# Changing when PV is held back beside full-array matmuls, the order of FFN blocks and two scheduler constants, in an attention + FFN kernel

## The chip, the cores and the metric

One core of a Trainium2 chip runs the whole program in one launch. The metric is device time in microseconds (us). Engines are named as in the profile: PE is TensorE's matmuls, PEld its weight loads, ACT is ScalarE, DVE is VectorE. "Before" and "after" are the two kernels. A ratio is the mean time of one kernel's fast runs over that of the other's fast runs of the same rounds, so it is not quite the ratio of the medians quoted.

## The reference, cut to what matters

```python
def reference(A_x, A_wqkv, A_wo, B_x, B_w1, B_b1, B_w2, B_b2):   # S=2048, D=1024, F=3584, 32 heads of 32
    q, k, v = split(layernorm(A_x) @ A_wqkv)
    p = softmax(q @ k.T * 32 ** -0.5)          # 32 heads x 2048 x 2048
    h = A_x + (p @ v) @ A_wo
    return h + gelu(layernorm(h) @ B_w1 + B_b1) @ B_w2 + B_b2
```

## The kernel before

The kernel isn't written in instruction order. It builds a graph of tasks, and a list scheduler with a cost table puts each engine's tasks in order at build time; that order is then fixed. Attention runs in eight chunks of 256 query rows. A chunk has eight *jobs* (one for each group of four heads), a job eight *rounds*. In a round PE makes eight score matmuls (QK, row-tiled, kind `qk`), ACT two exponentials, and PE eight PV matmuls and four of the softmax denominator (both column-tiled, kind `pv`). All other matmuls are *background*, in groups that need a PSUM bank each: first the K, Q and V projections, then per chunk the output projection (`wo`), `ffn1` of chunk c-1 and `ffn2` of chunk c-2. `ffn1` and the V projection run on the full array, most of the rest column-tiled.

```python
def round(self):                                   # one round of a job
    pe(fns, 0.217, ..., kind="qk", mode="row")     # scores of 8 matmuls
    act(... ACT.Exp ...)                           # twice; occ = EXP[q]
    pe(fns, 0.217, ..., kind="pv", mode="col")     # PV
    ...                                            # denominator, one round later
...
PLAN = [F2[0], 3, F2[1], 4, F2[2], 5, F2[3], 2]    # order of ffn2 groups and ffn1 blocks
...
pool_of = {7: [], 4: [], 6: B_ps[6].w + B_ps[6].r} # banks of jobs and background; 4 only in the lead-in
PV_START = 6
HOLD = 3

def full_array(t):                                 # ffn1 and V projections
    return t.alt is not None and t.grp.name[:2] in ("f1", "pv")

def pick_pe(rd, now, state, up):                   # what PE does next
    ...                                            # waiting: rounds whose P is ready and whose PV isn't done
    if qk is not None:
        return qk
    if pv is not None and not (state["mode"] == "full" and bg is not None and full_array(bg[1]) and waiting < HOLD):
        job = job_of.get(pv)
        if job is None or job.bank is not None:
            return pv
        if free and pv is pvs[n] and (waiting >= PV_START or last or bg is None):
            job.bank = free[0]                     # the job takes its PSUM bank here
            ...
            return pv
    if bg is not None:
        ...
        return t
```

The last-but-one group, ffn2 of chunk 6, can start only when all of chunk 6's ffn1 and its tanh have been placed.

The softmax here doesn't subtract the row's maximum and nothing guards it: scores larger than these inputs give would overflow.

## Time and profile before

| | before |
|---|---|
| time, median of three runs | 1099.68 us (1098.5 to 1100.67) |
| profiled span, mean granted clock | 1096.5 us, 0.997 |
| busy: PE, PEld, DVE, ACT | 1062.1, 589.0, 822.9, 1021.6 us |
| last QK starts, chunk 7's ffn1 starts | 1019.87, 1044.95 us |
| last matmul of chunk 6's ffn1 | 998.7 us |

The page has busy time per engine, the chain of work that ended last, and groups of instructions; the timeline lists an engine's instructions in order, with the idle time before each in brackets and what ended it. The lines themselves stand in the prediction.

### The profile page before, as it was taken

Reading aid. Unit: us, or ns where it says so; the run is one execution under the profiler, and the core shown is the slowest. Engines: PE = TensorE matmul, PEld = TensorE weight load, DVE = VectorE, ACT = ScalarE, POOL = GpSimd, SP = SyncE. Lnnn points to the kernel's source line nnn. Section 1 sums busy time; section 2 is a strip of 40 time slices with the busy share of each in tenths; the row PEclk is TensorE's granted clock in tenths of the full one; section 3 lists DMA queues with packets and bytes.
Section 4 is the critical chain, followed back from the end, with each engine's and each line's share of the span. In section 5 each row is a group of like instructions: output and inputs, shape, how many; then the busy total and the mean of one; then the engine's idle time right before and its main releaser. Section 6 shows DMA issues by size and latency. Waiting matters only on the chain.

```text
span 1096.5 us, 41949 instructions
## 1 busy us (share of the span) xinstructions
PE 1062.1 (97%) x19130; PEld 589.0 (54%) x19135; DVE 822.9 (75%) x1449; ACT 1021.6 (93%) x1135; POOL 17.8 (2%) x33
## 2 busy tenths in 40 slices
PE   7999999999999989999999999999999999999999
PEld 6545555554444655554555455455545544554485
DVE  7456666767767998788788788877887888887562
ACT  5889999999999999999999999999999999999351
POOL 1000000000000000000000000000000000000000
PEclk9999999999999999999999999999999999999999
DMA  7960100013444755577838856765778477968860
GB/s 197 195 159 3 51 3 3 3 41 92 120 122 127 210 133 162 183 242 150 271 113 254 218 169 185 210 208 153 234 162 255 136 224 205 311 186 261 248 224 20
DMA packets 269211, 176.52 MB, mean 161 GB/s; under 512 B 51434, under 2 KB 265066, under 8 KB 269034
## 3 DMA queue, kind: packets, MB, share of 16 engines
q1 hardware_dynamic: 269034, 173.84, 55.4%
q8 instruction: 150, 2.46, 0.9%
q14 instruction: 27, 0.22, 0.1%
HBM read 155.98 MB, written 11.01 MB: 152 GB/s over the span
## 4 chain that ended last, share of the span: by engine, by line
ACT 83%; PE 15%; DMA 1%; DVE 1%; issue 0%; POOL 0%; POOLq 0%; DVEq 0%
ACT PT L709 79%; PE ps L505 8%; ACT a_sq L850 4%; PE ps L502 3%; PE ps L701 1%; PE ps L721 1%; DMA hnT<-xb 1%; PE ps L907 1%; PE ps L740 1%; DVE PS L716 0%; ACT xnT L584 0%; PE ps L581 0%; DVE gT L851 0%; ACT V L592 0%; DVE a_os L878 0%
## 5 line engine op out<-in xcount | busy, mean ns | idle before, releaser
L709 ACT ACTIVATE PT<-ps 128x1024 bf16<-128x1024 f32 x1024 | 953.8, 1164 | 12.7 <-PE ps L701 12.4
L716 DVE TENSOR_TENSOR PS<-PT 128x1024 bf16<-128x1024 bf16 x495 | 327.6, 686 | 83.1 <-ACT PT L709 49.5
L701 PE MATMUL ps<-QT,KT 32*128 32x256 bf16 x4096 | 203.9, 273 | 13.5 <-ACT PT L709 11.5
L505 PE MATMUL ps<-hnT,w1r 128*128 128x256 bf16 x1632 | 209.5, 274 | 2.1 <-DVE gT L832 0.6
L502 PE MATMUL ps<-w2r,gT 128*32 128x512 bf16 x2880 | 192.8, 383 | 1.9 <-issue 0.8
L721 PE MATMUL ps<-PT,V 128*32 128x256 bf16 x4096 | 180.9, 275 | 5.9 <-ACT PT L709 5.0
L505 PEld LDWEIGHTS ps<-hnT,w1r 128*128 128x128 bf16 x1632 | 146.2, 98 | 57.0 <-issue 36.2
L701 PEld LDWEIGHTS ps<-QT,KT 32*128 32x128 bf16 x4096 | 61.3, 92 | 163.5 <-ACT PT L709 141.7
L740 PE MATMUL ps<-PS,ones 128*32 128x256 bf16 x1980 | 139.4, 276 | 2.3 <-DVE PS L716 1.5
L502 PE MATMUL ps<-xnT,Wall 128*32 128x512 bf16 x1888 | 126.0, 381 | 1.3 <-DVE stg L594 1.2
L721 PEld LDWEIGHTS ps<-PT,V 128*32 128x32 bf16 x4096 | 94.4, 96 | 54.5 <-ACT PT L709 24.0
L502 PEld LDWEIGHTS ps<-w2r,gT 128*32 128x32 bf16 x2880 | 67.4, 96 | 71.2 <-issue 26.7
L832 DVE TENSOR_TENSOR gT<-ps,b1f 128x512 bf16<-128x512 f32 x98 | 67.4, 687 | 25.7 <-PE ps L505 24.5
L740 PEld LDWEIGHTS ps<-PS,ones 128*32 128x32 bf16 x1980 | 51.7, 96 | 40.6 <-DVE PS L716 23.4
L505 PE MATMUL ps<-Wall,xnT 128*128 128x128 bf16 (+1 forms) x896 | 69.3, 227 | 0.7 <-ACT xnT L584 0.7
L851 DVE SCALAR_TENSOR_TENSOR gT<-a_sq,gT 128x1024 bf16<-128x1024 bf16 x49 | 59.9, 1222 | 12.3 <-ACT a_sq L850 11.8
L502 PEld LDWEIGHTS ps<-xnT,Wall 128*32 128x32 bf16 x1888 | 43.5, 96 | 46.5 <-issue 15.0
L505 PEld LDWEIGHTS ps<-Wall,xnT 128*128 128x128 bf16 x896 | 55.2, 98 | 16.3 <-issue 10.7
L502 PE MATMUL ps<-w1r,OT 128*32 128x512 bf16 x896 | 62.2, 381 | 0.5 <-DVE OS L752 0.2
L848 DVE SCALAR_TENSOR_TENSOR a_sq<-a_sq,gT 128x1024 bf16<-128x1024 bf16 x49 | 59.8, 1221 | 0.7
L850 ACT ACTIVATE a_sq<-a_sq 128x1024 bf16<-128x1024 bf16 x49 | 58.9, 1203 | 0.0
L749 DVE STREAM_TRANSPOSE DT<-ps 128x256 f32<-128x256 f32 x64 | 28.5, 445 | 20.1 <-PE ps L740 20.1
(76 smaller groups left out, 570.7 us busy)
## 6 DMA issues: line engine op xcount, KB each, us to landing
w2r<-in_B_w_dram SPq DMA_DIRECT2D x105, 512.0 KB, 6.0
w1r<-in_B_w_dram SPq DMA_DIRECT2D x102, 512.0 KB, 4.6
w1r<-in_A_wo_dram SPq DMA_DIRECT2D x28, 512.0 KB, 4.4
wk<-in_B_w_dram SPq DMA_DIRECT2D x9, 512.0 KB, 5.9
xrb<-in_A_x_dram SPq DMA_DIRECT2D x16, 256.0 KB, 4.9
Wall<-in_A_wqkv_dram SPq DMA_DIRECT2D x16, 256.0 KB, 5.1
wv<-in_B_w_dram SPq DMA_DIRECT2D x8, 512.0 KB, 6.9
a_x<-in_A_x_dram SPq DMA_DIRECT2D x28, 128.0 KB, 3.4
```

Source lines behind the costliest of these rows:

```text
L502: fns.append(lambda p, j=j: p.matmul(dst(32 * j, 32 * j + 32), lhsT[:, 32 * j:32 * j + 32], rhs, start=start, stop=stop, tile_position=(0, ...
L505: t.alt = [lambda p: p.matmul(dst(0, P), lhsT, rhs, start=start, stop=stop, skip_group_check=True)]
L701: fns.append(lambda p, i=i, hh=hh, r0=r0: p.matmul(psum[:, 2 * us[hh // 2] + hh % 2, 256 * i:256 * i + 256], KT[r0:r0 + 32, g, 256 * r + P ...
L709: t = act(lambda a, u=u, q=q: a.activation(PT[:, s, 2 * q:2 * q + 2, :], psum[:, 2 * u:2 * u + 2, :], ACT.Exp, bias=0.0, scale=SCALE), 102 ...
L716: dve(lambda v: v.tensor_tensor(PS[:, z, :, :], PT[:, s, :, 0:256], PT[:, s, :, 256:512], ALU.add), c_dve(1024, 2), reads=B_PT[s], writes= ...
L721: fns.append(lambda p, i=i, hh=hh: p.matmul(psum[32 * hh:32 * hh + 32, self.bank, 0:256], V[:, g, 2 * r + i, 32 * hh:32 * hh + 32], PT[:, ...
L740: fns.append(lambda p, i=i, hh=hh, src=src: p.matmul(psum[32 * hh:32 * hh + 32, self.bank, 256:512], ones32[:, :], src[:, hh, :], start=False,
L749: dve(lambda v: v.transpose(DT[f][:], psum[:, self.bank, 256:512]), c_dve_ps(256), reads=[self.buf], writes=[B_DT[f]], prio=-1)
L832: gate[c] = dve(lambda v, xh=xh, fc=fc, grp=grp: v.tensor_tensor(xh, psum[:, grp.bank, :].rearrange("p (f n) -> p f n", f=2), b1f[:, fc:fc ...
L848: dve(lambda v: v.scalar_tensor_tensor(v4(sq), v4(sq), C2, xh, ALU.add, ALU.mult), c_dve(n), reads=[b_sq] + b_xh, writes=[b_sq], prio=GP)
L850: gate[c] = act(lambda a: a.activation(sq, sq, ACT.Tanh, bias=0.0, scale=K2 / 2), n, writes=[b_sq], prio=-1, kind="tanh")
L851: t = dve(lambda v: v.scalar_tensor_tensor(xh, v4(sq), 1.0, xh, ALU.add, ALU.mult), c_dve(n), reads=[b_sq] + b_xh, writes=b_xh, prio=GP)
```

## The change

Its intent, in its author's words: PV is held back while a full-array ffn1 group has work, until three rounds of P wait, so that PV runs in longer column-tiled stretches. Four lines differ (three edits: the *rule*, the *plan*, and the *constants* of the cost table).

```diff
-    EXP = (0.9163, 0.9013)
+    EXP = (0.9161, 0.9011)
...
-    PLAN = [F2[0], 3, F2[1], 4, F2[2], 5, F2[3], 2]
+    PLAN = [F2[0], 2, F2[1], 6, F2[2], 5, F2[3], 1]
...
-        if pv is not None and not (state["mode"] == "full" and bg is not None and full_array(bg[1]) and waiting < HOLD):
+        if pv is not None and not (bg is not None and not last and full_array(bg[1]) and waiting < HOLD):
...
-    gr.schedule(pick_pe, switch=0.11382196630878494)
+    gr.schedule(pick_pe, switch=0.10231147062341138)
```

## The prediction

> **What bounds the kernel now.** I read four views: the busy table and clock, the chain of waits, every ACT idle gap, and the PE timeline where chunks change.
>
> ```profile
> PE 1062.1 (97%) x19130; PEld 589.0 (54%) x19135; DVE 822.9 (75%) x1449; ACT 1021.6 (93%) x1135; POOL 17.8 (2%) x33
> ...
> ACT 83%; PE 15%; DMA 1%; DVE 1%; issue 0%; POOL 0%; POOLq 0%; DVEq 0%
> ...
> L709 ACT ACTIVATE PT<-ps 128x1024 bf16<-128x1024 f32 x1024 | 953.8, 1164 | 12.7 <-PE ps L701 12.4
> ```
>
> PE and ACT both look full, but 83% of the chain that ended last is ACT, nearly all of it the softmax exponentials. They waited only 12.7 us in total. The ACT timeline says where these gaps lie: after the exponential that starts at 63.26 us only four gaps over 0.05 us remain before the exponentials end: 0.28, 0.39, 0.88 and 1.40 us, 2.95 us together. (The others lie in the first 63 us, in the lead-in, which the changed rule doesn't touch: its matmul groups are named neither ffn1 nor V projection.) Two of these gaps and the end of attention:
>
> ```profile
> 818.93 21.20 ACT L709 ACTIVATE PT<-ps 128x1024 bf16<-128x1024 f32 x23 [0.88 <-PE ps L701]
> 1009.56 11.11 ACT L709 ACTIVATE PT<-ps 128x1024 bf16<-128x1024 f32 x12 [1.40 <-PE ps L701]
> ```
>
> So from 63 to about 1022 us ACT sets the pace: 330 exponentials took 302.67 us in the chain (63.26 to 366), 0.917 us each. The change removes no exponential. After 1022.5 us the bound is PE. The tail, by the PE timeline:
>
> ```profile
> 1023.48 0.81 PE L505 MATMUL ps<-wk,OT 128*128 128x512 bf16 x3 [0.16 <-issue]
> ...
> 1030.25 1.89 PE L505 MATMUL ps<-w2r,gT 128*128 128x512 bf16 x8
> 1031.97 0.61 PE L581 MATMUL ps<-ident,xbl 128*128 128x128 bf16 x8
> 1032.42 2.97 PE L505 MATMUL ps<-w2r,gT 128*128 128x512 bf16 x12
> 1035.22 0.61 PE L581 MATMUL ps<-ident,xbl 128*128 128x128 bf16 x8
> 1035.67 9.44 PE L505 MATMUL ps<-w2r,gT 128*128 128x512 bf16 x42
> 1044.95 1.91 PE L505 MATMUL ps<-hnT,wk 128*128 128x256 bf16 x16
> ```
>
> The reader sees the last output projection (1023.48 to 1030.25), then 62 matmuls of the second FFN product (ffn2) of chunk 6, left over from attention, then ffn1 of chunk 7 from 1044.95. The ACT timeline has the last hnT copy at 1035.87, 1.02 us long, so ffn1 could start at 1036.89. The leftover is useful filler up to there; behind it, 1044.95 - 1036.89 = 8.06 us are pure backlog on the path. **This 8 us and the 2.95 us of ACT gaps are all that PE scheduling can give back.** The rest of the tail, ffn1 and ffn2 of chunk 7, is back-to-back full-array work.
>
> [...]
>
> ```profile
> 1014.50 0.33 PE ps L701 x8
> 1014.83 1.41 PE ps L502 x24
> 1016.24 0.33 PE ps L701 x8
> 1016.57 1.62 PE ps L502 x28
> 1018.19 0.33 PE ps L701 x8
> 1018.52 0.55 PE ps L502 x8
> 1019.07 0.44 PE ps L721 x16
> ```
>
> Eight PV matmuls (L721, column-tiled, behind column-tiled ffn2) take 0.44/2 = 0.22 us; eight QK matmuls (L701, row-tiled, 256 columns too) between column-tiled ones take 0.33, so one change costs 0.11 us. The ffn2 pieces confirm it: 28 less 24 is 0.21 for four, so eight should take 0.42 and take 0.55 after QK. [...] The trace has 917, and I use 917: ACT has no slack hidden between its instructions. [...] PE's 97% is not proof that PE is the bound; the chain decides, and it says ACT until 1022.
>
> **The change, part by part.** No instruction is added or removed; the order on PE changes, and with it DMA and DVE order. The diff has four edits.
>
> (1) The rule. Before, a ready PV was held back only when PE stood in full-array mode. QK comes once a round, every two exponentials (1.83 us), puts PE in row mode, and so lets PV through right behind it. Once in column mode, PV drained until none was left. After, PV is held in any mode while a full-array ffn1 or V-projection group is next and fewer than three rounds of P wait. Read literally, this removes the after-QK visits with one or two rounds waiting, but also removes the hysteresis: after one PV the count falls from 3 to 2 and the hold is on again. A job (8 rounds) still starts only at six waiting. Before, it drains six and then takes one or two more visits. After, it drains four, and then gets one round at a time. The PE records of the last chunk (905 to 1023 us) hold 134 mode changes and 13 column stretches of PV or its denominator alone beside ffn1: 5 between row and full (10.5 rounds of PV), 4 between full and row, 4 between two QKs. After the change I count, as an estimate: 224 ffn1 matmuls of 0.1095 us (1.91 us for 16 in the tail timeline, less overlap: 1.75/16) are 24.5 us, at about 1.2 us of free PE time a round some 20 rounds, up to one visit each. A visit in the middle of ffn1 costs two changes, one behind QK only one. Worst case 40 changes against about 20 now: 20 x 0.11 = **+2.2 us** of PE time in the last chunk. If the visits merge as intended, some 6 to 10 fewer: **-0.7 to -1.1 us**.
>
> (2) The order. PV yields to ffn1, so ffn1 of chunk 6 can end earlier by the PVs deferred: two to three rounds of PV and denominator at 0.33 us, 0.7 to 1.0 us. This matters, because ffn2 of chunk 6 may start only when the last tanh of ffn1 has been placed: ffn1's last matmuls start at 997.58, the tanh at 1004.21, ffn2 at 1004.86; in between PE had only attention, with waits of 0.29, 0.41, 0.52 and 0.41 us (1.63 in all). The deferred PVs fill these. Worth **-0.7 to -1.6 us** of the 8 us backlog.
>
> (3) The plan of blocks, from 3, 4, 5, 2 to 2, 6, 5, 1. Now the first three ffn1 blocks alternate with pieces of ffn2 (16 ffn1 matmuls, then 4 to 12 of ffn2, three times at 929 to 937 us). One block fewer in that place takes out one alternation, 2 to 4 changes: **-0.2 to -0.4 us**. The last ffn1 pair ends at about the same time.
>
> (4) The constants of the scheduler's cost tables (exponential 0.2 ns shorter, mode change 0.102 for 0.114) cost nothing on the chip, but can flip ties anywhere. This is luck of placement: 1 or 2 us either way.
>
> Only what falls in the last chunk moves the end by the backlog; in earlier chunks PE time hides beside ACT, as the four small gaps show. Sum with the middle of each: (1) between +2.2 and -0.9, say +0.5; (2) -1.1; (3) -0.3; ACT gaps 2.95 us, of which I let a third be recovered, -1. That is -1.9 us. From the median 1099.68 I predict **1097.8 us**.
>
> **The rivals.** *A: visits multiply.* PE needs 2 to 4 us more, the backlog of 8 us grows to 12, and QK is sometimes late: 1103 to 1105 us. For it: the missing hysteresis; against it: PE still has waits of 1.63 us in the last chunk, and attention work has first call. *B: the backlog goes.* Changes fall enough to put 4 to 8 us more of ffn2 ahead of attention's end: 1090 to 1094 us. For it: 134 changes x 0.11 = 14.7 us of the last chunk are changes, so a tenth fewer is 1.5 us; against it: two changes per QK can't go, and QK is most of them (64 rounds). *C: nothing visible.* ACT hides all of it, within 1.5 us of now. *D: ACT starves on P slots.* Eight slots of P, six of which wait when a job starts; PV held longer keeps two more filled and its PSUM bank occupied for some two rounds more, so a late bank would stop exponentials. For it: 0.88 us of gap already at 818.93 with column work before it; against: the hold ends at three waiting, well under eight. It would make 1105 to 1115 us.
>
> **Range and chances.** C and a weak B are likeliest; A next. The floor, if all backlog and all gaps went, is 1099.68 - 8.06 - 2.95 = 1088.7, which is 1.0% below: faster by over 2% (1077.7) is out of reach unless ACT itself gets quicker. Slower by over 2% (1121.7) needs 22 us, which only D could make. Range 1091.5 to 1103.5 us; faster 0.01, within 2% 0.975, slower 0.015.
>
> **What would show it right or wrong.** Exponentials still 0.917 us and their gaps after 63 us under 4 us in sum: the bound stands. Mode changes in the last chunk counted from the PE records: below 134 is the intent, above is A. The start of chunk 7's ffn1 after the end of the last hnT copy: under 8.06 us is gain, over it loss, and the total should move by that plus the shift of attention's end. ffn2 of chunk 6 should start 1 us or so earlier against the end of ffn1. The prediction is wrong if ACT gains gaps over 5 us, if the tail after the last QK shrinks by more than the backlog, or if the lead-in's 63 us move.

The price of a mode change is read from the fence of seven lines (1014.50 to 1019.07 us), and the 917 ns are the 302.67 us of 330 exponentials.

## More of the kernel before

Scores use six of the eight PSUM banks that the kernel allocates (`B_ps`), so after the lead-in two banks are left, 6 and 7. An open job holds one of them until its result is copied out, and background groups then share the other.

Time differences in the experiments are differences of the two medians, unless a profile's span is named.

## The result

After took **1103.69 us** (median of four, 1103.22 to 1104.29), before 1099.74 (1098.5 to 1100.67): ratio 1.0037, interval 1.002 to 1.0054. That is "within 2%", as forecast, but 0.2 us above the range, and slower where I had said faster.

The page of after, the three lines that answer to the first fence of the prediction:

```profile
PE 1063.7 (97%) x19126; PEld 591.2 (54%) x19126; DVE 821.8 (75%) x1449; ACT 1022.9 (93%) x1135; POOL 16.9 (2%) x33
...
ACT 66%; PE 32%; DVE 1%; issue 1%; POOL 0%; DVEq 0%; POOLq 0%
...
L709 ACT ACTIVATE PT<-ps 128x1024 bf16<-128x1024 f32 x1024 | 952.8, 1123 | 14.4 <-PE ps L701 14.0
```

Busy times are the same within 2.2 us: no work came or went. But PE's share of the chain that ended last is 32% in place of 15%: the exponentials often depend on PE now. The ACT timeline of after between 400 and 460 us, where before shows no gap of this kind:

```profile
417.69 1.02 ACT L709 ACTIVATE PT<-ps 128x1024 bf16<-128x1024 f32 x1 [0.61 <-PE ps L701]
421.64 1.06 ACT L850 ACTIVATE a_sq<-a_sq 128x1024 bf16<-128x1024 bf16 x1 [0.15 <-DVE a_sq L848]
425.76 6.65 ACT L709 ACTIVATE PT<-ps 128x1024 bf16<-128x1024 f32 x7 [0.32 <-PE ps L701]
445.88 7.50 ACT L709 ACTIVATE PT<-ps 128x1024 bf16<-128x1024 f32 x8 [0.60 <-PE ps L701]
```

Three of these wait for QK and one for DVE; more gaps before exponentials follow at 604, 647, 807 and 840 us. The end, from after's PE timeline:

```profile
1028.16 1.04 PE L505 MATMUL ps<-wk,OT 128*128 128x512 bf16 x4
...
1035.15 1.89 PE L505 MATMUL ps<-w2r,gT 128*128 128x512 bf16 x8
...
1037.33 2.54 PE L505 MATMUL ps<-w2r,gT 128*128 128x512 bf16 x11
...
1040.15 10.52 PE L505 MATMUL ps<-w2r,gT 128*128 128x512 bf16 x48
1050.51 1.91 PE L505 MATMUL ps<-hnT,wk 128*128 128x256 bf16 x16
```

The last output projection starts at 1028.16 (before 1023.48), and 67 matmuls of leftover ffn2 follow (before 62). The last hnT copy ends at 1041.37 (its ACT record: 1040.35, 1.02 us long), so the backlog on the path is 1050.51 - 1041.37 = 9.14 us (before 8.06). From the start of chunk 7's ffn1 to the end both take 51.6 us.

So the profiled span grew by 5.6 us: attention ends later (last exponential starts at 1026.18, before 1021.33: +4.85), the stretch from there to the end of the last hnT copy is 0.37 shorter, and the backlog is 1.08 larger. The 4.85 splits by the ACT records into three. The first exponential after the lead-in starts 1.47 later. The gaps after it sum to 4.96 us in place of 3.00 (+1.96). The remaining 1040 operations took 919.7 ns each in place of 918.3 (+1.4: waits too short to show as gaps). Of after's gaps, those at 418, 422, 426, 446, 604, 647, 807 and 840 us came back in its control run e1 within 0.5 us of their place (all gaps of e1 sum to 4.4 us); what e14, the control of before, shows stands below.

### The profile page after: what moved, and what is told of

Its sections match the earlier page's. It is cut to its first block, busy times and chain, and to the rows that moved or that the text cites. A ratio compares the mean times of both kernels' runs of the same rounds, so it can differ in the third digit from the quotient of the medians.

```text
span 1102.1 us, 41919 instructions
## 1 busy us (share of the span) xinstructions
PE 1063.7 (97%) x19126; PEld 591.2 (54%) x19126; DVE 821.8 (75%) x1449; ACT 1022.9 (93%) x1135; POOL 16.9 (2%) x33
## 3 DMA queue, kind: packets, MB, share of 16 engines
q8 instruction: 150, 2.46, 0.9%
## 4 chain that ended last, share of the span: by engine, by line
ACT 66%; PE 32%; DVE 1%; issue 1%; POOL 0%; DVEq 0%; POOLq 0%
ACT PT L709 62%; PE ps L502 11%; PE ps L505 11%; PE ps L701 4%; ACT a_sq L850 3%; PE ps L721 3%; PE ps L740 2%; PE ps L907 1%; DVE stg L594 0%; DVE PS L716 0%; ACT xnT L584 0%; DVE a_sq L848 0%; DVE gT L851 0%; PE ps L581 0%; DVE gT L832 0%
## 5 line engine op out<-in xcount | busy, mean ns | idle before, releaser
L709 ACT ACTIVATE PT<-ps 128x1024 bf16<-128x1024 f32 x1024 | 952.8, 1123 | 14.4 <-PE ps L701 14.0
L505 PE MATMUL ps<-hnT,w1r 128*128 128x256 bf16 x1632 | 214.3, 275 | 4.5 <-DVE gT L832 2.5
L721 PEld LDWEIGHTS ps<-PT,V 128*32 128x32 bf16 x4096 | 98.2, 96 | 49.6 <-ACT PT L709 20.4
L505 PE MATMUL ps<-Wall,xnT 128*128 128x128 bf16 (+1 forms) x896 | 72.2, 229 | 2.8 <-DVE V L594 1.9
L749 DVE STREAM_TRANSPOSE DT<-ps 128x256 f32<-128x256 f32 x64 | 28.5, 445 | 20.6 <-PE ps L740 20.5
```

The costliest lines, as they stand in the source:

```text
L505: t.alt = [lambda p: p.matmul(dst(0, P), lhsT, rhs, start=start, stop=stop, skip_group_check=True)]
L709: t = act(lambda a, u=u, q=q: a.activation(PT[:, s, 2 * q:2 * q + 2, :], psum[:, 2 * u:2 * u + 2, :], ACT.Exp, bias=0.0, scale=SCALE), 102 ...
L721: fns.append(lambda p, i=i, hh=hh: p.matmul(psum[32 * hh:32 * hh + 32, self.bank, 0:256], V[:, g, 2 * r + i, 32 * hh:32 * hh + 32], PT[:, ...
L749: dve(lambda v: v.transpose(DT[f][:], psum[:, self.bank, 256:512]), c_dve_ps(256), reads=[self.buf], writes=[B_DT[f]], prio=-1)
```

## The experiments

All kernels gave correct results. Two theories stood at the start. **Theory 1, background work left undone:** the time follows how much background matmul work is still undone when attention ends, plus ACT gaps. **Theory 2, mode changes:** each change of tiling mode costs 0.11 us (in before, the first matmul of a new mode ends 0.21 us after the last of the old one with 256 columns, and 0.32 with 512, where 0.108 and 0.2155 are usual); the program of after has 1255, that of before 1215 (the single PE records agree with the program). A third, chance in the clock, was to be told apart by controls. The background work done by a given moment is worked out from the PE records: each matmul counted at 0.2155 us per 512 columns, the usual step from end to end in the records (half for 256, a quarter for each column-tiled piece), and compared with the first profile of before at the same round of attention (round 512 is the last).

### The three edits alone, and the control

**e1_after_again** is after unaltered; **e2_rule_only**, **e3_plan_only** and **e4_constants_only** are before with one edit each, as in the diff above.

> The changed kernel unaltered, as a control: how far do its lead-in, its clock dips and its gaps repeat? Theory 1 (backlog and ACT gaps): 3.5 to 4.5 us over the kernel before, of which about 1.7 us is backlog (the program has 77 matmuls of chunk 6's ffn2 behind the last QK, 69 before; 8 x 0.2155) and 1.5 to 2 us ACT gaps that repeat at the same places (418, 426, 446, 647, 807, 840 us). Theory 2 (mode changes): its 40 more changes cost 4.4 us. Theory 3 (clock dips, chance): lead-in 1.5 us longer than before only in the first profile, not here, and 2 to 3 us over before.

> Only the hold rule, with the old plan and constants. The program has 112 matmuls of chunk 6's ffn2 behind the last QK (all four groups) in place of 69, and 1273 mode changes in place of 1215. Theory 1: +43 x 0.2155 = +9.3 us, so about 1109. Theory 2: +58 x 0.11 = +6.4 us at most, about 1106. If the rule as such is harmless and the plan or constants did the harm: 1098 to 1101.

> Only the plan 2, 6, 5, 1, with the old rule and constants. 102 matmuls behind the last QK (+33), 1196 mode changes (-19). Theory 1: +33 x 0.2155 = +7.1 us, about 1107. Theory 2: -2 us or nothing. The two differ in sign here.

> Only the two constants of the cost tables, with the old rule and plan. 75 matmuls behind the last QK (+6), 1206 mode changes (-9). Theory 1: +1.3 us, 1101, plus or minus what the ACT gaps do. Theory 2: -1 us.

| run | median us | before in the same rounds | ratio (interval) |
|---|---|---|---|
| e1 after again | 1102.29 | 1097.73 | 1.0040 (1.0022 to 1.0057) |
| e2 rule | 1116.95 | 1097.73 | 1.0176 (1.0157 to 1.0194) |
| e3 plan | 1112.09 | 1097.73 | 1.0123 (1.0104 to 1.0142) |
| e4 constants | 1106.03 | 1097.73 | 1.0070 (1.0054 to 1.0086) |

Each edit alone is *worse* than all three together. Theory 2 falls: plan and constants have 19 and 9 fewer mode changes and are 14.4 and 8.3 us slower. Theory 1 has the signs right and the sizes too small (+9.3, +7.1 and +1.3 expected from the program, +19.2, +14.4 and +8.3 measured). The traces say why. When the matmuls of each chunk's ffn1 were through, in us:

| ffn1 of chunk | 0 | 1 | 2 | 5 | 6 | last QK |
|---|---|---|---|---|---|---|
| before | 397.0 | 490.1 | 589.6 | 896.4 | 998.7 | 1019.9 |
| after | 405.1 | 504.6 | 606.2 | 906.0 | 1005.6 | 1024.7 |
| e1 after again | 405.1 | 504.7 | 606.2 | 905.6 | 1005.3 | 1024.4 |
| e2 rule only | 410.8 | 509.0 | 611.4 | 920.2 | 1025.3 | 1019.4 |
| e3 plan only | 397.3 | 491.4 | 591.4 | 891.6 | 1012.0 | 1024.0 |

With the rule, ffn1 is already 8 to 14 us late at its *first* chunk and stays late to the end. In background work: the rule alone is 3.5 us behind before at round 128, 7.6 at round 192 (the end of the projection stage, with most of chunk 0's ffn1 done too), 12.0 at round 288, and still 13.0 at the last QK. A lag made early need not be hidden beside ACT.

It isn't that PE has no time to spare. Behind chunk 0's ffn1, PE of before has no background matmul for 9.2 us:

```profile
396.65 0.61 PE L505 MATMUL ps<-hnT,w1r 128*128 128x256 bf16 x4
...
406.16 2.67 PE L505 MATMUL ps<-hnT,w1r 128*128 128x256 bf16 x17
```

In between it does attention's matmuls and waits for exponentials; the next chunk's ffn1 needs an hnT that is filled again only when this ffn1 is through. In after the same hole lies from 405.1 to 415.85. At round 202, inside it, after, e9 and e10 have made good all of their lag. When ffn1 ends late, the hole and all behind it start late, so that after is 5.4 us behind again at round 206 and 7.3 at round 256. Nor is a lag always carried to the end: after is 1.0 us behind at round 448. e5, which differs from it by the plan alone, is 7.9 behind there, so the new plan pays this back. But attention of after is then 6.0 us late itself.

In e2 ffn1 of chunk 6 then isn't through when attention ends, and ffn2 of chunk 6 can't fill the wait for the last layer norm. From its PE timeline:

```profile
1022.70 2.90 PE L505 MATMUL ps<-hnT,w1r 128*128 128x256 bf16 x25
1025.44 1.03 PE L505 MATMUL ps<-wk,OT 128*128 128x512 bf16 x4
...
1036.19 1.03 PE L581 MATMUL ps<-ident,xbl 128*128 128x128 bf16 x8 [1.82 <-DVE xbl L574]
1037.02 19.91 PE L505 MATMUL ps<-w2r,gT 128*128 128x512 bf16 x80
1056.77 0.93 PE L505 MATMUL ps<-hnT,wk 128*128 128x256 bf16 x7
```

ffn1 of chunk 6 ends behind the last QK (1019.37), PE idles, and all of ffn2 of chunk 6 lies on the path: 18.5 us from the last hnT copy to the next ffn1, before 8.06. In e3 the loss is in the last chunk. Its background was 1.6 us *ahead* of before at round 448 and is 7.1 behind at the last QK; PE's idle gaps from round 448 to the last QK sum to 13.2 us, before 5.3.

### Pairs

**e5_rule_constants** has rule and constants with the old plan, **e6_plan_constants** is after without the rule, **e13_rule_plan** has rule and plan with the old constants. With these all eight combinations are measured.

> Rule and constants, old plan. Theory 1 (the time follows how much background matmul work is still undone when the last QK is issued, plus gaps): 112 matmuls of chunk 6's ffn2 left in the program (before 69), so at least +9.3 us, 1107 to 1113. It shares its program with the changed kernel up to the middle of chunk 3's attention, so the lag of background work at round 192 should again be 3.6 us, not the 7.6 of the rule alone. Theory 2 (mode changes, 62 more x 0.11): +6.8 us. The clock dip at 20 us seen in both profiles of the changed kernel should be here too if the program makes it; it is chance if it isn't here.

> The changed kernel without the rule. If the rule is what makes the changed kernel slow, this one is at 1097 to 1099. Theory 1: 84 left in the program (+15 x 0.2155 = +3.2 us), and the last chunk idles on PE as in the plan-only and constants-only runs (rest of 15 to 20 us after round 448 in place of 10), so 1104 to 1109, slower than the changed kernel: the rule then doesn't cost, it pays back part of what plan and constants lose. Theory 2: 17 fewer mode changes, 1096.

> Rule and plan, old constants. Program: 1277 mode changes, all 112 matmuls left. Lag theory: projection stage identical to the rule alone (lag 7.6 us at round 192), ffn1 of chunk 6 ends behind attention, so 1112 to 1120. Additive effects of the edits (1.76% + 1.23%): 1130. If plan mends what the rule does: under 1104.

| combination | ratio | sum of the single effects |
|---|---|---|
| rule + plan (e13, 1131.15 us, fast runs) | +3.07% | +2.99% |
| rule + constants (e5, 1109.63 us) | +1.20% | +2.46% |
| plan + constants (e6, 1111.72 us) | +1.33% | +1.93% |
| all three (e1, 1102.29 us) | +0.40% | +3.69% |

Rule and plan add up, as the expectation of e13 had it for that case; its lag theory, with 1112 to 1120 us, missed. The constants, bad on their own, mend most of what the other two do. So the question "what did the rule cost?" has no single answer: +1.76% on top of before, and -0.93 percentage points on top of plan and constants (e6 to e1). The expectation of e6 had that sign, but stopped at 1109; its ACT gaps came to 11.2 us. e5 shares after's first rounds and has the same lag at round 192, 3.6 us; its lead-in has no clock dip, so the dip at 20 us of after (one half for 3.4 us from 19.88 us, by its clock records) isn't made by the program. One of e13's four executions, the profiled one, took 1969 us with PE slow throughout (its records make PE busy for 1939.7 us, before 1062.1, at a recorded clock of 1.00); I have no explanation, and leave its profile out. The other three lie between 1130.6 and 1132.1.

That single effects don't add up is largely in the programs. Run on a host without the chip, the scheduler of each kernel ends with a span by its own cost table (`gr.span`): 1084.6 for before, 1083.7 for after, 1100.6, 1090.8 and 1083.6 for rule, plan and constants alone, 1112.2 for rule and plan. So in the model the whole change wins 0.9 us, where its single effects sum to +21; it could have been asked before the forecast. It has no clock drops, and against before the chip adds 3 to 13 us to what it says of the other seven combinations.

### Where and how the rule makes background late

**e7_rule_v_only** applies the rule beside V projections only. **e8_true_drain** builds the stated intent: once three rounds wait, PV drains to zero.

```diff
 # e7: the new condition only for groups named "pv" (V projections), the old one else
+        if pv is not None and not (bg is not None and (state["mode"] == "full" or (not last and ... grp.name[:2] in ("pv",))) and full_array(bg[1]) and waiting < HOLD):
 # e8
+    def hold(waiting, state, bg, last):
+        if waiting >= HOLD:
+            state["drain"] = True
+        elif waiting == 0:
+            state["drain"] = False
+        return bg is not None and not last and full_array(bg[1]) and not state["drain"]
```

> The rule applied only where the next background group is a V projection; beside ffn1 the old rule stands. If the rule's harm is done in the projection stage, the background lag at round 192 is 7 us as with the whole rule, and stays about there to the end: 1108 to 1116. If it is done beside ffn1 (the stage I predicted for), the lag at round 192 is under 2 us and the time under 1104.

> The stated intent, really built: PV is held beside a full-array group until three rounds of P wait, and then drains until none waits (a flag keeps the drain on). 1204 mode changes in place of 1273 with the rule as written (before 1215). If the lost drain is what makes the rule slow PE down, the background lag at round 192 is at most 2 us (rule as written: 7.6). If holding PV as such does it (its PSUM bank kept longer, background groups short of banks), it is 5 us or more. The end of the program has 112 left, so the time is still some 9 us over before in both cases.

e7: 1109.97 us against 1097.28, ratio 1.0116 (1.0096 to 1.0135). Its lag at round 192 is 7.2 us, and 9.3 at the last QK. So with the old plan and constants most of the rule's harm is done beside the V projections, where I hadn't looked. e8: 1119.54, ratio 1.0203 (1.0182 to 1.0224), 22 us over before where some 9 were expected. With 11 *fewer* mode changes in the whole program and 8 fewer by round 192 it lags 6.4 us there. I had half believed that the lost drain was the fault (the count falls from three to two after one PV, and PV stops). The program order shows that this does happen:

```diff
 # PE order where the two first differ, beside a V projection: before, with - the lines that the rule takes out
 L721 PV x8
-L740 denominator x4
-L721 PV x8
-L740 denominator x4
-L721 PV x8
-L740 denominator x4
-L721 PV x8
 L505 V projection
```

but e8 shows that restoring the drain doesn't bring the time back. What is left of the theories is that PV held at all leaves a job's PSUM bank occupied for longer. From the start of a job's first PV to the copy of its result took 6.61 us on average in the projection stage before, 7.84 with the rule alone, 7.31 in e8 and 8.13 in after. With one bank left, each background group must wait until DVE has emptied the bank of the one before it. PE's own waits between 90 and 385 us (engine, line, what it waited for: us in total, times, longest), before:

```profile
PE ps L701 <- ACT PT L709: 1.6, 4, 0.8
PE ps L502 <- DVE stg L594: 1.2, 3, 0.6
...
PE ps L721 <- DVE stg L594: 0.2, 1, 0.2
PE ps L502 <- DVE OS L752: 0.2, 1, 0.2
```

and after:

```profile
PE ps L505 <- DVE V L594: 1.9, 4, 0.6
PE ps L502 <- DVE stg L594: 1.6, 5, 0.4
PE ps L701 <- ACT PT L709: 0.7, 3, 0.3
PE ps L502 <- DVE KT L594: 0.6, 1, 0.6
PE ps L502 <- DVE QT L594: 0.6, 1, 0.6
```

Waits for DVE to empty a bank of a projection (L594) or of a job's result (L752) were 1.6 us before. In after the four such rows shown sum to 4.7, and all such rows to 5.6. The releasers say whose copy a bank waited for.

Waits for a bank aren't the whole lag. In e2 all such rows sum to only 3.4 us, with a lag of 7.6. Summed from the single PE records between rounds 20 and 192, PE idled 2.7 us more than before in after, 3.4 in e2 and 4.9 in e8. After has 24 more mode changes there, worth 2.6 us at 0.11, e2 17 more (1.9), e8 8 fewer. So in after itself mode changes cost about as much as idle time. And e2 and e8 get from round 20 to 192 in 1.9 and 1.8 us less time, which counts as lag too.

**e9_no_hold** drops the hold altogether, **e10_hold_four** is the rule with `HOLD = 4`.

> No hold at all: PV runs as soon as it is ready once its job has a PSUM bank (old plan and constants). Bank theory (a job that stays open keeps one of the two banks that background groups use): jobs are open for no longer than before (mean 6.6 us in the projection stage, against 7.8 with the rule alone), so the background lag at round 192 is 2.5 us or less although the program has 9 more mode changes by there. Drain theory (a broken drain costs): lag of 5 us or more. The end of the program leaves 112 matmuls, so the time is worse than before in any case, 1107 or more.

> The rule as written, but PV waits for four rounds of P in place of three (old plan and constants). The program has the same number of mode changes in the projection stage as before (458 against 459, the rule alone 477). Bank theory: jobs stay open longer still (over 8.5 us in the projection stage) and the background lag at round 192 is 8 us or more. Mode-change theory: no lag there.

e9: 1120.87, ratio 1.0221. Jobs are open 6.65 us in the projection stage and the lag at round 192 is 2.8 us, near what was expected; then, beside ffn1, it grows to 14.8 us by round 288, with 40 more mode changes by there. So holding PV beside ffn1 is worth having, and the old rule was a good one. e10: 1123.02, ratio 1.0240. Jobs are open 8.79 us, the program has as many mode changes as before by round 192, and the lag there is 4.7 us. Mode changes alone, which said no lag, are refuted again as the only cause. But I had expected 8 us or more. Over all runs open time and lag do not rank alike (after: 8.13 us and 3.6; e2: 7.84 and 7.6). Longer open jobs go with a lag in every one of these runs (though not in e16, below), but the size isn't explained by them alone.

### Holding PV before its job opens

If an open job is what costs, PV should be held *before* it takes the bank. **e11_start_seven** is before with that one number changed, **e12_start_seven_exp** adds calibrated constants, **e15_start_seven_const** the new constants, and **e16_start_seven_all** is the whole change with it.

```diff
-    PV_START = 6
+    PV_START = 7
 # e12 also: EXP = (0.917, 0.917), switch=0.108
```

> The kernel before with one number changed: a job takes its PSUM bank when seven rounds of P wait in place of six. PV is held where holding costs no bank, before its job opens. Bank theory: jobs open 5 to 6 us in place of 6.6, 30 fewer mode changes, background ahead of before by 2 us or more at round 192, and 65 matmuls left in the program in place of 69: 1094 to 1098, at or below before. Rival: P has eight slots, seven now wait, so exponentials stall: ACT gaps over 10 us and 1105 or more.

> As the run before it, with the scheduler's exponential set to the 0.917 us that the traces show, and its mode change to 0.108: 1179 mode changes, 56 matmuls left. Bank theory: 13 x 0.2155 = 2.8 us less backlog than before, so 1092 to 1097. Rival: as there.

> A job's bank taken at seven waiting rounds, with the new constants. Program: 1202 mode changes, 56 matmuls left (before 69). Two-term account (shift of the last QK plus background left undone): -2.8 us from the backlog, plus what the ACT gaps do, 3 us as with start at seven alone: 1096 to 1101. If the ACT gaps are of that program only: 1093 to 1096.

> The whole change with a job's bank taken at seven waiting rounds. Program: 1239 mode changes, 64 matmuls left. Against the changed kernel: 13 fewer left, -2.8 us, and jobs open shorter in the projection stage (7.5 us or less against 8.1), lag at round 192 at most 3 us; ACT gaps perhaps 2 us more: 1098 to 1103.

| run | ratio (interval) | background at round 192, us | ACT gaps, us (before 3.0) | last QK, us against before |
|---|---|---|---|---|
| e11 | 1.0048 (1.0031 to 1.0064) | 0.5 ahead | 6.1 | +3.5 |
| e12 | 1.0081 (1.0063 to 1.0099) | 5.8 ahead | 10.8 | +11.2 |
| e15 | 1.0084 (1.0068 to 1.0101) | 4.0 ahead | 10.4 | +9.0 |
| e16 | 1.0030 (1.0015 to 1.0044) | 2.3 ahead | 3.2 | +3.6 |

e16 against after is the cleanest test of the cause. The rule, plan and constants are those of after. Jobs are open 7.11 us instead of 8.13 in the projection stage, and the lag of 3.6 us at round 192 becomes a lead of 2.3. It has 17 fewer mode changes by there, which at 0.11 are 1.9 of these 5.9 us. PE's waits for a bank, all rows, are 1.6 us as before, in place of 5.6. So relieving the bank does relieve background. But no time follows: 1.0030 and 1.0040 can't be told apart by their intervals. The rival of e11's expectation was right in kind, if not in size: ACT gaps grew, in all but e16. e11 itself says little about the bank, since its jobs are open no shorter (6.60 us, expected 5 to 6). In e12 background led by 14.8 us at round 384 and the last QK came 11.2 us later. None of these beat before; e11, e12 and e15 came out 4, 9 and 6 us above the range that their expectations gave.

### The same program twice: how much is the clock

**e14_before_again** is before, unaltered.

> The kernel before, unaltered. If its program makes its gaps: ACT gaps at 536, 741, 819 and 1009.6 us again, ffn1 of chunk 6 ending at 998.7 within 1.5 us, backlog of 8.1 us behind the last hnT copy within 0.5, clock dips near 404 and 1004.8 us. If they are chance, dips and gaps elsewhere, or the lead-in 1.5 us longer with a dip near 20 us as in the changed kernel. Time within 0.15% of before.

1096.92 us, ratio 1.0001. The profile's program is the same, its span 1093.9 in place of 1096.5 us. The backlog is again 8.06 and ffn1 of chunk 6 ends at 997.7, but of the four ACT gaps only the one near 819 returned (now 1.27 us). The windows show why. Columns: stretch, length, busy time of PE, PEld, DVE, ACT and POOL, then the granted PE clock and DMA. The first profile of before:

```profile
1000.00:1010.00 10.00, 8.38 (x164) 3.72 (x156) 6.87 (x10) 8.60 (x10) 0.00 (x0) 0.83 0.84 250
```

and e14:

```profile
1000.00:1010.00 10.00, 8.38 (x172) 3.42 (x164) 7.74 (x13) 10.00 (x12) 0.00 (x0) 1.00 0.85 249
```

A mean of 0.83 in 10 us is a clock of one half for 3.4 us; the clock records put it at 1004.84 us in the first profile, and e14 has none there. (An earlier drop, at 404.09 us, returned in e14 at 403.53.) What PE did just before, in stretches of 3.4 us; the first profile, where both stretches end at a drop:

```profile
400.69:404.10 3.41, 1.79 (x40) 0.72 (x40) 2.77 (x5) 3.41 (x5) 0.00 (x0) 1.00 0.61 169
...
1001.40:1004.80 3.40, 1.78 (x44) 0.69 (x40) 2.73 (x4) 3.40 (x5) 0.00 (x0) 1.00 1.14 319
```

Where such a stretch begins is not free: in each of the 17 profiles all drops start whole multiples of 3.4133 us from each other, within 0.01 us (the two in before are 600.746 us apart, 176 times that; the two in after 392.533, 115 times). Counted on from its drop at 403.53, e14's stretch here is this one, without a drop:

```profile
1000.86:1004.27 3.41, 2.08 (x50) 0.80 (x46) 2.39 (x3) 3.41 (x5) 0.00 (x0) 1.00 1.16 305
```

PE is out of background in both, in the hole behind chunk 6's ffn1. But in the first profile one whole stretch lies in the hole, with PE busy for 1.78 us of 3.40, and the clock drops; in e14 the stretches lie otherwise over the same program, and this one has 2.08 us and doesn't end in a drop. The drop made the 1.40 us gap that I had counted as recoverable. In e14 the last QK came 2.6 us earlier, of which 1.0 had been gained by round 448. All clock records that aren't cut by the end of a trace and aren't full are one half for 3.4, 6.8 or 10.2 us (in before 3.4 twice, in after 3.4 and 6.8). PE wasn't idle through the stretch before a drop: in before's two it did attention's matmuls, and was busy for 1.79 and 1.78 of 3.4 us. At what share of busy time the clock halves isn't shown. The first profiles of before and after alone would part the stretches at full clock (1.79 us or less with a drop behind them, 1.93 or more without), but over all 17 profiles those that ended in a drop had PE busy for 0.72 to 2.38 us, and others without a drop as little as 1.72.

Over the recorded fast runs of before the time goes with the granted clock: 16 runs at 0.998 average 1095.3 us, 13 at 0.995 1098.3, 8 at 0.994 1099.8; all 46 with a recorded clock lie between 1094.7 and 1100.4. After had ten runs in the result and in e1: none above 0.995. Five at 0.995 average 1103.0 and three at 0.994 1102.2. At equal clock after is thus 2.4 to 4.7 us slower; the rest of the difference goes with its lower mean clock. Its dip at about 412 us is 6.8 us long in both profiles, before's at about 404 us 3.4 in both. Four of its ACT gaps, at 418 to 446 us, follow that dip, which starts in the hole behind chunk 0's ffn1. Its dip at 20 us, with which the lead-in is 1.5 us longer, occurs in other runs with the old constants as well (e9 and e10) and not in e5, which shares its lead-in: that one is chance.

### The account over all runs

Two numbers from a trace place every run: how much later the last QK starts, and how much background work is undone there, both against the first profile of before.

| run | last QK | undone | sum | span |
|---|---|---|---|---|
| after | +4.8 | +1.7 | +6.5 | +5.6 |
| e2 rule | -0.5 | +13.0 | +12.5 | +18.8 |
| e3 plan | +4.1 | +7.1 | +11.2 | +10.3 |
| e4 constants | +4.9 | +1.3 | +6.2 | +5.3 |
| e6 plan, constants | +9.4 | +3.2 | +12.6 | +12.0 |
| e7 rule beside V | +0.8 | +9.3 | +10.1 | +11.2 |
| e8 drain | -3.6 | +18.9 | +15.3 | +20.5 |
| e12 start 7, exp | +11.2 | -2.8 | +8.4 | +8.6 |
| e14 before again | -2.6 | 0.0 | -2.6 | -2.6 |

The sum is within 1.2 us of the span in these rows, and within 2.1 in those left out (e15 is the farthest), save for e2 and e8 (6.3 and 5.2 more), and likewise e9 and e10: in just these four ffn1 of chunk 6 ends behind the last QK, and the tail has waits of its own.

## Why the prediction was wrong

**What held.** The bound in the main: ACT has 66% of the chain that ended last (before 83%), and after the last exponential it is PE. But the prediction's own test of it, gaps under 4 us after 63 us, failed with 4.96. The price of a mode change entered the account unchanged. The tail's shape was right: its full-array part took 51.6 us in both. The floor argument ("faster by over 2% is out of reach") stands. Rival A named 1103 to 1105 us, where the result lies, and its reason in part: the program has 40 more changes. But they are elsewhere: in its last 64 rounds there are 149, before 148 (the 134 is right for 905 to 1023 us, a shorter stretch), and the backlog grew by 1.1 us, not by 4.

**The step that failed** is the sentence that let me size the last chunk alone: "in earlier chunks PE time hides beside ACT". It made the sum -0.9 us of backlog, from (1) to (3), and -1 us of ACT gaps. The runs show +1.08 us of backlog and, for the term that I had at -1, attention ending 4.85 us later: 1.47 in the lead-in, 1.96 in gaps and 1.4 in shorter waits. Most of the miss is thus exponentials that wait for QK in earlier chunks, not the tail. (The lead-in's part goes with the clock drop at 20 us and is chance. The rule doesn't touch it, as I wrote, but the constants do: PE's order is another from round 8 on.)

**Part (2)**, "ffn1 of chunk 6 can end earlier ... 0.7 to 1.0 us", failed with it. ffn1 ended 6.9 us *later* (998.7 to 1005.6), and its ffn2 started at 1012.5 in place of 1004.86. About 6 of the 6.9 us are attention's own lateness there (6.2 us at round 500); counted in rounds, ffn1 ended behind QK of round 502 in place of 501. So the deferred PVs didn't bring it forward, but the debt of the first chunks was nearly paid.

**Part (1)**, the visits, was sized at 0.5 us for the last chunk, beside ffn1. With the old plan and constants most of the rule's harm is done in the projection stage beside the V projections (e7: +1.16% by that alone). And the cost isn't mode changes alone (e8 has fewer and lags 6.4 us), but also PV held after its job has opened. I had written under rival D that a job's "PSUM bank [is] occupied for some two rounds more", and then charged it to ACT. The traces charge a part of it to the background groups that need the bank (5.6 us of waits in after, 1.6 before).

**Part (3)**, the plan, was -0.2 to -0.4 us for one alternation fewer. Alone it is +1.23%: it starves PE in the last chunk (13.2 us of idle gaps, before 5.3). **Part (4)**, "1 or 2 us either way" for the constants, was too small by a factor of four: +0.70% from shifting an assumed exponential by 0.2 ns and a mode change by 12 ns, with another PE order from round 8 on, where the first tie flips. **The sum** then added the four parts. Three of the four sums measured, all that include the constants, are far from additive (3.69% expected of the three, 0.40% measured).

**The ACT gaps**, of which I let 1 us be recovered: the largest of the four, 1.40 us, was a clock drop that comes and goes (one half for 3.4 us from 1004.84 us; e14 has neither the drop nor the gap).

What stays open: what makes each late exponential of after late, beyond the four gaps that follow a clock drop; why the lag doesn't follow open time in size; and why a program whose background runs ahead (e12, e15) is late with its exponentials. Two readings of the last were not tested: that more background is then ready to sit in front of QK, and that the queue runs empty sooner. For the second, the traces have longer holes without background (13.2 us from 996.8 us in e12, 8.4 from 800.5 in e15) with a clock drop in each, and 20.5 and 23.9 us of halved clock after the lead-in, before 6.8.

## What to carry to other kernels

Where a bound engine hides another's work, ask whether the hidden engine can use its spare time *when it has it*, and not only whether it is waited for: here it had 9 us without background behind chunk 0's ffn1, and a delay in front of this hole moved all behind it. Work held back while it holds a buffer takes that buffer from others; taking the bank later (e16) removed the lag, though not the time. And in a kernel whose order comes from a tuned list scheduler, single edits aren't causes that add up: measure the combinations, or first ask the scheduler's own model, and size "ties that flip" from that before forecasting tenths of a per cent.
